# Hash attention with a channel mix: the hash signs of two head pairs made in one PSUM bank

## The chip, the cores and the metric

The kernel runs on one core of a Trainium2 chip. The metric is the device time of one execution in microseconds (us). The engines are named as in the profile: PE is the matrix engine (PEld its weight loads), DVE the vector engine, ACT the scalar engine, POOL the GpSimd engine, SP the engine whose queue issues most transfers; ACTq, POOLq and SPq are the queues of these engines.

## What is computed

The reference has two stages. The first is attention over 4 batches, 8 heads, 768 tokens and 64 values a head, with a hash mask: q and k are projected on 6 directions, the 6 signs make a bucket, and a query sees only keys of its own bucket.

```python
q_bits = (np.einsum('bhsd,dk->bhsk', q, proj) > 0)      # 6 signs
mask = q_bucket[:, :, :, None] == k_bucket[:, :, None, :]
scores = np.where(mask, scale * np.matmul(q, k.transpose(0, 1, 3, 2)), -1000000000.0)
attn = softmax(scores);  out = np.matmul(attn, v)
```

The second is a channel mix over the 512 columns of all heads: each token is mixed with the one before it (`xk`, `xr`), then `k = relu(xk @ w_k)`, `v = (k*k) @ w_v`, `r = sigmoid(xr @ w_r)`, and the output is `r * v`. In what follows "FFN" is this second stage.

## The kernel before

**Pairs, slots, and the order of work.** Two heads of one batch are a pair: 16 pairs, numbered 0 to 15, four to a batch. A pair has 12 slots: for each of its heads j, 6 chunks of 128 keys. The loop over G (line 714) writes the order of all engines out by hand, with n the pair and s its slot: a score of the chunk (`score`, line 421: two matmuls of 384 columns into PSUM, one exp on ACT that writes `pt`), the PV product of the chunk two slots back (`pv`, line 442, six matmuls into `oo`), then half of the slot's FFN work, then what the slot has of side work, then the other half of the FFN work. FFN work is a queue of single matmuls with costs, fed at a fixed rate (`ffn`, line 630); the FFN of a batch begins in slot 5 of the fifth pair (pairs 4, 8, 12) and its outputs leave some three to four pairs later. `later(k, fn)` puts work off to the beginning of the slot k further on. Every engine works off its own instructions in this order, so one that waits holds up all behind it on the same engine, and SP's queue is such a queue too.

**How the mask gets into the scores.** The signs, as +0.5 and -0.5, stand as 6 more rows under the 64 rows of q and k (tiles `aq` and `ak`, called `au` in the code, 70 rows), so that the score matmul adds a term that is greatest for equal buckets. Three sets of these tiles turn round over the pairs (`NSET`, line 199).

**From q and k to signs, for pairs 6 to 15.** Pairs 0 to 5 are loaded and turned in another way (`load_qk`, `turn`, `bits`, with signs at line 388 and their transfers at line 394), which the change leaves as it is. For pairs 6 to 15, four steps count:

- `load_blocks(n + 3)` (line 259) in slot 1 of pair n (slot 3 in pair 4, slot 6 in pair 3): 16 transfers on SP, issued at lines 271, into one of two buffers `blk`; `load_v` (line 278) stands just ahead of it. A `blk` buffer comes free when the squares on ACT (`norm`, line 287, slots 8 and 10 of the pair before) have read it.
- `turn_blocks(n + 2)` (line 326): one transpose for q and one for k on DVE (line 330) into `tq` and `tk`, one buffer each, and four casts on POOL (lines 340 and 342) into the 64 upper rows of `aq` and `ak`. It is done in slots 4 and 5 of pair n, or 6 and 7 where n is a multiple of four.
- `bits_blocks(n + 2, "A")` (line 350) in slot 10 of pair n: four matmuls in 32-bit floats with the projection `projp` as weights, each into 32 rows of a PSUM bank; the rows of head j stand at 6j in a group of 32. `projp` holds the projection twice: for the upper 64 rows in columns 0 to 5, for the lower 64 in columns 6 to 11.
- Its `rest`, at the beginning of slot 11: one comparison on DVE from the bank into `sg` (line 366) and eight transfers on SP (line 371) of six rows each into `aq` and `ak`. The first score that reads them comes 13 slots after the block.

**Banks.** Two PSUM tiles of two banks take scores by turns; four more banks, A to D, take all else. From pair 4 on, C and D belong to the FFN, A and B to the two heads' outputs `oo`: A from slot 2 to 7 of a pair, B from slot 8 to slot 1 of the next. In between, `turn_out` (line 473, slot 3) turns the output of the pair before with six PE transposes into bank B, DVE copies it out into `xt` (line 480), and a shifted column block is copied within `xt` on POOL (line 485; on DVE for the last pair of a batch). The mix of tokens (`mix`, line 490, on DVE) reads `xt` in slots 8 and 9 (slot 4 at a batch's end). Bank A holds the sign block in slots 10 and 11.

Of the kernel before, what the change touches and what calls it, by code (L numbers as in the profile page):

```python
# [9 lines left out]
FP32 = mybir.dt.float32  # L10
BF16 = mybir.dt.bfloat16
# [5 lines left out]
P = 128  # L17
# [12 lines left out]
def kernel(  # L30
# [13 lines left out]
    nc = tc.nc  # L44
    B, H, S, D = q.shape
    NB = proj.shape[1]
# [3 lines left out]
    HALF = S // 2  # L50
    NDC = DM // P
    NFC = DF // P
    NPB = H // 2
    NPAIRS = B * NPB
    AUG = D + NB

    consts = ctx.enter_context(tc.tile_pool(name="consts", bufs=1))
# [5 lines left out]
    nc.vector.memset(epsm, EPS)  # L63
    expb = consts.tile([P, 1], FP32, name="expb")
    nc.vector.memset(expb, EXP_BIAS)
    projp = consts.tile([P, 32], FP32, name="projp")
    nc.vector.memset(projp, 0.0)
    nc.scalar.dma_start(out=projp[0:D, 0:NB], in_=proj)
    nc.vector.tensor_copy(projp[D:P, NB : 2 * NB], projp[0:D, 0:NB])
    make_identity(nc, ident16)  # L70
# [97 lines left out]
    def fast():  # L168
        with ExitStack() as fx:
            pool = lambda nm, bufs, **kw: fx.enter_context(  # L170
                tc.tile_pool(name=nm, bufs=bufs, **kw)
            )

            NKEEP = NPB + 2
            nat = pool("nat", 1)
            blkp = pool("blk", 2)
            turnp = pool("turn", 1)
            vfp = pool("vf", 3)
            sgp = pool("sg", 2)
            sqp = pool("sq", 1)  # L180
            vap = pool("va", 1)
            ptp = pool("pt", 6)
            obp = pool("ob", 2)
            rcp = pool("rc", 4)
            xtp = pool("xt", 1)
# [13 lines left out]
            NSET = 3  # L199
            augs = []  # L200
# [26 lines left out]
            def later(k, fn):  # L227
                due.append((clock[0] + k, len(due), fn))
# [120 lines left out]

            def bits_blocks(n, which):  # L350

                au = augs[n % NSET]
                groups = [(side, e) for e in range(2) for side in "qk"]
                bb = bank(which, [P, HALF], FP32, f"bb{n}")
                for g, (side, e) in enumerate(groups):
                    nc.tensor.matmul(  # L356
                        bb[32 * g : 32 * g + 32, :],
                        projp,
                        turned[n, side][:, e * HALF : (e + 1) * HALF],
                        start=True,  # L360
                        stop=True,
                    )

                def rest():
                    sg = sgp.tile([P, HALF], BF16, name=f"sg{n}", tag="sg")
                    nc.vector.tensor_scalar(
                        out=sg, in0=bb, scalar1=0.0, scalar2=0.5, op0=ALU.is_gt, op1=ALU.subtract
                    )
                    for j in range(2):
                        for g, (side, e) in enumerate(groups):  # L370
                            nc.sync.dma_start(
                                out=au[side, j][D:AUG, e * HALF : (e + 1) * HALF],
                                in_=sg[32 * g + NB * j : 32 * g + NB * j + NB, :],
                            )

                later(1, rest)

            def bits(n, js, which, two_queues=False):
                au = augs[n % NSET]
# [19 lines left out]
            def values(n, j):  # L399
                vf = vfs[n][:, j, :]  # L400
                va, vs = vsets[n % NSET][j]
                if n < NSET:
                    nc.gpsimd.memset(va[:, :, D : D + 1], 1.0)
                    nc.gpsimd.memset(vs[:, D : D + 1], float(NC_))
                if n < NKEEP:
                    nc.gpsimd.tensor_copy(
                        va[:, :, 0:D].rearrange("p (e c) d -> p e c d", e=2),
                        vf.rearrange("p (c e d) -> p e c d", e=2, d=D),
                    )
                else:  # L410
                    nc.gpsimd.tensor_copy(
                        va[:, :, 0:D], vf.rearrange("p (c d) -> p c d", d=D)
                    )
                s3 = sgp.tile([P, 3 * D], FP32, name=f"s3{n}_{j}", tag="s3")
                nc.gpsimd.tensor_add(s3, vf[:, 0 : 3 * D], vf[:, 3 * D : 6 * D])  # L415
                nc.gpsimd.tensor_add(s3[:, 0:D], s3[:, 0:D], s3[:, D : 2 * D])
                nc.gpsimd.tensor_add(vs[:, 0:D], s3[:, 0:D], s3[:, 2 * D : 3 * D])
                vas[n, j], vss[n, j] = va, vs
# [268 lines left out]
                out=mu_rows[NDC : 2 * NDC, :], in_=moe_mu_r.rearrange("(c p) -> c p", p=P)  # L687
            )
            values(0, 0)
            turn(1, 0, 0, "B")  # L690
            turn(1, 1, 0, "D")
            values(0, 1)
# [21 lines left out]
            for G in range(nslots + LAG):  # L714
                clock[0] = G
                n, s = divmod(G, 12)
                live = G < nslots
                run_due()

                if live and s == (5 if n == 0 else 6 if n == NPB - 1 else 3 if n <= NPB else 1):  # L720
                    if NPB <= n < NPAIRS - 2:
                        load_v(n + 2)
                    if n + 3 < NPAIRS:
                        (load_qk if n + 3 < NKEEP else load_blocks)(n + 3)
                    if n < NPB:
                        load_v(n + 2)
                w = weights.get(n, {}).get(s)
                if w:
                    if w[0] == "v":
                        load_wv(w[1])  # L730
                    else:
                        load_w(*w)
                old = chunks[G - LAG] if G >= LAG else None
                first = old is not None and old[2] == 0
                if live:
                    score(*chunks[G])
                if old and not first:
                    pv(*old, oo_bank(*old[:2]))
                rate = 25.9 / (NPB * 12 + (3 if n >= NPAIRS - NPB else 0))
                ffn(rate / 2)  # L740
                mb = misc_bank(n, s)
                if live:
                    if n == 0:
                        if s in (0, 1):
                            turn(1, s, 1, "BD"[s])
                    if n == 1 and s == 0:
                        mups = bank(mb, [P, 2 * NDC], FP32, "mups")
                        nc.tensor.transpose(mups, mu_rows, ident32[0 : 2 * NDC, 0 : 2 * NDC])
                        nc.vector.tensor_copy(mu_sb, mups)
                    if s == (3 if n == 0 else 1) and n + 1 < NKEEP:  # L750
                        bits(n + 1, (0, 1), mb)
                    if s == 10 and NKEEP <= n + 2 < NPAIRS:
                        bits_blocks(n + 2, "A")
                    if s == 3 and n >= 1:
                        turn_out(n - 1, mb)
                    if n >= NPB:
                        if s == 4 and n % NPB == 0:
                            mix((n - 1) // NPB, (n - 1) % NPB, 0)

                        if s in (8, 9) and n % NPB:  # L760
                            mix((n - 1) // NPB, (n - 1) % NPB, 0, [(0,), (1, 2)][s - 8])

                    ms = (5, 7, 9) if n == NPB - 1 else (6, 8, 10)
                    if s in ms and 1 <= n < NPB:
                        mix(0, n - 1, 0, [ms.index(s)])

                    xs = [NPB * 12 + x for x in (5, 10, 11, 12)]
                    if G in xs:
                        mix(0, xs.index(G), 1)
                    if n > NPB and s == (10 if n % NPB else 5):  # L770
                        mix((n - 1) // NPB, (n - 1) % NPB, 1)
                    if s in (5, 7, 9, 11) and n + 2 < NKEEP:
                        x = (s - 5) // 2
                        turn(n + 2, x % 2, x // 2, mb)
                    ts = (6, 7) if n % NPB == 0 else (4, 5)
                    if s in ts and NKEEP <= n + 2 < NPAIRS:
                        turn_blocks(n + 2, ts.index(s))
                    vs_ = (6, 10) if n < NPB else (0, 2)
                    if s in vs_ and n + 1 < NPAIRS:
                        values(n + 1, vs_.index(s))  # L780
                    if s in (8, 10) and NKEEP <= n + 2 < NPAIRS:
                        norm(n + 2, (s - 8) // 2)
                ffn(rate / 2)
                if old and first:
                    pv(*old, oo_bank(*old[:2]))
                if live and n >= NPB and n % NPB == 0 and s == MIXSLOT - 1:
                    queue.extend(ffn_items(n // NPB - 1))
# [178 lines left out]
    with tc.manual_schedule():  # L966
        fast()
# [33 lines left out]
```

## Time and profile before

| What | Value |
|---|---|
| median of 3 runs | 267.44 us (266.5 to 267.85) |
| the profiled execution | 267.24 us |
| its span, first to last instruction | 265.4 us |
| mean granted PE clock | 0.996 of full speed |
| first score of pair 0 / 5 / 6 / 7 / 8 | 12.3 / 68.7 / 84.4 / 98.6 / 113.3 us |
| first score of pair 9 / 11 / 13 / 15 | 127.9 / 157.1 / 186.2 / 213.2 us |
| moved over the span | 36.50 MB, 138 GB/s |

Times within an execution count from the span's start. The span falls into a start-up of 12.3 us, four pairs without FFN work (some 11 us each), pairs 4 to 15 with it, and an end of some 40 us after pair 15 in which the last batch's FFN runs alone. In the profile, each instruction is named by its engine, line and operation, with the tiles that it writes and reads, as in `bb<-tq,projp`; a busy matrix engine is not one at its peak, as its instructions overlap. A "wait" names the instruction whose end let a waiting engine go on.

### The profile page before, as it was taken

Reading aid. Unit: us, or ns where it says so; the run is one execution under the profiler, and the core shown is the slowest. Engines: PE = TensorE matmul, PEld = TensorE weight load, DVE = VectorE, ACT = ScalarE, POOL = GpSimd, SP = SyncE. Lnnn points to the kernel's source line nnn. Section 1 sums busy time; section 2 is a strip of 40 time slices with the busy share of each in tenths; the row PEclk is TensorE's granted clock in tenths of the full one; section 3 lists DMA queues with packets and bytes.
Section 4 is the critical chain, followed back from the end, with each engine's and each line's share of the span. In section 5 each row is a group of like instructions: output and inputs, shape, how many; then the busy total and the mean of one; then the engine's idle time right before and its main releaser. Section 6 shows DMA issues by size and latency. Waiting matters only on the chain.

```text
span 265.4 us, 6612 instructions
## 1 busy us (share of the span) xinstructions
PE 248.4 (94%) x2411; PEld 150.1 (57%) x2441; DVE 186.0 (70%) x378; ACT 213.8 (81%) x318; POOL 124.5 (47%) x248
## 2 busy tenths in 40 slices
PE   7799999999989999999999999998999999989990
PEld 5366657566555655565565656564656666545450
DVE  3667689889898775759588776778596645776440
ACT  2099979799989998979999997988999988179700
POOL 5787597770999471913665484706392000000000
PEclk9999999999999999999999999999999999999998
DMA  6548685857759292959665391959510002220042
GB/s 218 201 85 165 246 311 124 252 120 168 188 113 240 37 236 50 245 151 235 169 168 115 86 199 51 220 183 227 133 59 8 2 2 82 79 79 0 19 148 86
DMA packets 25976, 36.50 MB, mean 138 GB/s; under 512 B 3144, under 2 KB 21136, under 8 KB 25936
## 3 DMA queue, kind: packets, MB, share of 16 engines
q1 hardware_dynamic: 24008, 32.45, 47.2%
q0 software_dynamic: 1536, 3.15, 5.3%
q8 instruction: 21, 0.34, 0.6%
q10 hardware_dynamic: 392, 0.40, 0.5%
q14 instruction: 19, 0.16, 0.2%
HBM read 30.68 MB, written 6.29 MB: 139 GB/s over the span
## 4 chain that ended last, share of the span: by engine, by line
PE 56%; DVE 14%; DMA 11%; ACT 7%; SPq 5%; issue 4%; ACTq 0%; DVEq 0%
PE vp L529 14%; PE sc L427 13%; PE kp L529 10%; PE oo L454 7%; PE rp L529 5%; ACT pt L434 5%; DMA blk<-in_k_dram 4%; SPq L394 3%; DMA qk<-in_k_dram 3%; DMA qk<-in_q_dram 2%; PE bb L356 2%; PE ot L479 2%; SPq L271 2%; DVE xk L511 2%; DMA blk<-in_q_dram 2%
## 5 line engine op out<-in xcount | busy, mean ns | idle before, releaser
L434 ACT ACTIVATE pt<-sc,expb 128x768 bf16<-128x768 f32 x192 | 166.2, 909 | 26.3 <-PE sc L427 15.8
L427 PE MATMUL sc<-aq,ak 70*128 70x384 bf16 x384 | 93.9, 325 | 2.4 <-DMA aq<-sg 0.3
L454 PEld LDWEIGHTS <-pt 128*128 128x128 bf16 x1152 | 60.5, 97 | 26.7
L454 PE MATMUL oo<-va,pt 128*128 128x65 bf16 x1152 | 66.3, 193 | 0.0
L529 PE MATMUL kp<-xk,wk_sb 128*128 128x384 bf16 x256 | 55.6, 325 | 2.2 <-DVE kr L554 1.1
L427 PEld LDWEIGHTS <-ak 70*128 70x128 bf16 x384 | 34.9, 98 | 28.7 <-issue 7.4
L529 PE MATMUL vp<-wv_sb,k 128*128 128x512 bf16 (+1 forms) x187 | 48.9, 370 | 0.4
L561 DVE TENSOR_TENSOR k<-kr 128x384 bf16<-128x384 bf16 x64 | 28.5, 460 | 6.6 <-ACT kr L552 6.1
L529 PEld LDWEIGHTS <-wk_sb 128*128 128x128 bf16 x256 | 21.7, 97 | 14.3 <-issue 4.0
L340 POOL CAST aq<-tq 64x768 bf16<-64x768 f32 x20 | 16.6, 832 | 23.4 <-PE sc L427 11.7
L529 PE MATMUL rp<-wr_sb,xr 128*128 128x512 bf16 x79 | 24.5, 379 | 0.7 <-issue 0.2
L552 ACT ACTIVATE kr<-kp 128x384 bf16<-128x384 f32 x36 | 18.1, 503 | 7.4 <-PE kp L529 7.4
L529 PEld LDWEIGHTS <-k 128*128 128x128 bf16 x200 | 16.8, 97 | 12.8 <-issue 2.7
L485 POOL COPY xt<-xt 128x127 bf16<-128x127 bf16 x12 | 3.5, 294 | 41.8 <-DVE xt L480 41.8
L415 POOL TENSOR_TENSOR s<-vf 128x192 f32<-128x192 f32 x32 | 22.0, 688 | 0.0
L593 DVE SCALAR_TENSOR_TENSOR os<-th,vp 128x512 f32<-128x512 bf16 (+1 forms) x25 | 16.5, 662 | 6.9 <-PE vp L529 5.8
L465 DVE RECIPROCAL rc<-oo 128x6 f32<-128x6 f32 x32 | 6.1, 190 | 20.5 <-PE oo L454 20.5
L480 DVE COPY xt<-ot 128x768 bf16<-128x768 bf16 x16 | 8.9, 557 | 16.0 <-PE ot L479 16.0
L554 DVE TENSOR_SCALAR kr<-kp 128x384 bf16<-128x384 f32 x28 | 15.4, 550 | 6.3 <-PE kp L529 6.1
L466 DVE TENSOR_TENSOR ob<-oo,rc 128x384 bf16<-128x384 f32 x32 | 17.8, 557 | 1.1
L342 POOL TENSOR_SCALAR ak<-tk 64x768 bf16<-64x768 f32 x20 | 17.1, 854 | 2.8 <-DVE tk L330 1.3
L298 ACT ACTIVATE sq<-blk 128x768 bf16<-128x768 f32 x20 | 17.0, 852 | 0.0
(72 smaller groups left out, 308.2 us busy)
## 6 DMA issues: line engine op xcount, KB each, us to landing
blk<-in_q_dram SPq DMA_DIRECT2D x40, 176.0 KB
blk<-in_k_dram SPq DMA_DIRECT2D x40, 176.0 KB
vf<-in_v_dram SPq DMA_DIRECT2D x16, 384.0 KB
out_dram<-os SPq DMA_DIRECT2D x23, 256.0 KB
wvs<-in_moe_w_v_dram SPq DMA_DIRECT2D x4, 512.0 KB
qk<-in_q_dram SPq DMA_DIRECT2D x3, 384.0 KB
qk<-in_k_dram SPq DMA_DIRECT2D x3, 384.0 KB
aq<-sg SPq DMA_DIRECT2D x64, 4.5 KB
```

The source lines that it names most:

```text
L298: nc.scalar.activation(junk.rearrange("p (u d) -> p u d", u=NTOK), blks[n][:, i, :, 0:32], AF.Square, scale=1.5, accum_out=nrm[:, i, n : n ...
L340: eng.tensor_copy(dst, src)
L342: eng.tensor_scalar(out=dst, in0=src, scalar1=ALPHA, scalar2=1.0, op0=ALU.mult, op1=ALU.mult,)
L415: nc.gpsimd.tensor_add(s3, vf[:, 0 : 3 * D], vf[:, 3 * D : 6 * D])
L427: nc.tensor.matmul(sc[:, sp, 0:HALF], au["k", j][:, jc * P : (jc + 1) * P], au["q", j][:, sp * HALF : (sp + 1) * HALF], start=True, stop=True,
L434: nc.scalar.activation(pt.rearrange("p (s q) -> p s q", s=2), sc[:, :, 0:HALF], AF.Exp, bias=expb, scale=SCALE,)
L454: nc.tensor.matmul(oo[:, ic, :], pts[n, j, jc][:, ic * P : (ic + 1) * P], vas[n, j][:, jc, :], start=False, stop=(jc == NC_ - 1 and ic == ...
L466: nc.vector.tensor_tensor(out=obs[n][:, :, j * D : (j + 1) * D], in0=oo[:, :, 0:D], in1=rc.to_broadcast([P, NC_, D]), op=ALU.mult,)
L529: nc.tensor.matmul(box["t"], lhs(), rhs(), start=(i == 0), stop=(i == len(mms) - 1))
L552: nc.scalar.activation(kr, kp, AF.Relu)
L561: lambda: nc.vector.tensor_tensor(out=k2, in0=kr, in1=kr, op=ALU.mult),
L593: nc.vector.scalar_tensor_tensor(out=os_, in0=mx["th", b, c][:, ms], scalar=1.0, in1=vp, op0=ALU.add, op1=ALU.mult,)
```

## The change

There is a second weight tile `projq`, zero but for columns 16 to 27, which hold what `projp` has in columns 0 to 11. In slot 5 of an odd pair n, `bits_blocks(n + 1)` makes the signs of pairs n+1 and n+2 in bank B: four matmuls with `projp` for pair n+1, then four with `projq` for pair n+2 that add to the same bank, so that the second pair's rows stand 16 further down in each group of 32. There is one comparison for both, at the beginning of slot 6, followed by the eight transfers of pair n+1; those of pair n+2 follow in two lots of four, 5 and 9 slots after the block. For that, `turn_blocks(n + 2)` moves to slots 1 and 2 where n is odd; where n is even it stays. The buffers of `tq` and `tk` are doubled, those of `vf` go from three to two and those of `pt` from six to five.

```diff
     projp = consts.tile([P, 32], FP32, name="projp")
+    projq = consts.tile([P, 32], FP32, name="projq")
     nc.vector.memset(projp, 0.0)
+    nc.vector.memset(projq, 0.0)
...
-            turnp = pool("turn", 1)
-            vfp = pool("vf", 3)
+            turnp = pool("turn", 2)
+            vfp = pool("vf", 2)
...
-            ptp = pool("pt", 6)
+            ptp = pool("pt", 5)
...
             def bits_blocks(n, which):
 
-                au = augs[n % NSET]
+
                 groups = [(side, e) for e in range(2) for side in "qk"]
                 bb = bank(which, [P, HALF], FP32, f"bb{n}")
-                for g, (side, e) in enumerate(groups):
-                    nc.tensor.matmul(
-                        bb[32 * g : 32 * g + 32, :],
-                        projp,
-                        turned[n, side][:, e * HALF : (e + 1) * HALF],
-                        start=True,
-                        stop=True,
-                    )
+                for m in range(2):
+                    for g, (side, e) in enumerate(groups):
+                        nc.tensor.matmul(
+                            bb[32 * g : 32 * g + 32, :],
+                            (projp, projq)[m],
+                            turned[n + m, side][:, e * HALF : (e + 1) * HALF],
+                            start=(m == 0),
+                            stop=(m == 1),
+                        )
+                sg = sgp.tile([P, HALF], BF16, name=f"sg{n}", tag="sg")
 
                 def rest():
-                    sg = sgp.tile([P, HALF], BF16, name=f"sg{n}", tag="sg")
                     nc.vector.tensor_scalar(
                         out=sg, in0=bb, scalar1=0.0, scalar2=0.5, op0=ALU.is_gt, op1=ALU.subtract
                     )
-                    for j in range(2):
-                        for g, (side, e) in enumerate(groups):
-                            nc.sync.dma_start(
-                                out=au[side, j][D:AUG, e * HALF : (e + 1) * HALF],
-                                in_=sg[32 * g + NB * j : 32 * g + NB * j + NB, :],
-                            )
+                    send(0, 0)
+                    send(0, 1)
+
+                def send(m, j):
+                    au = augs[(n + m) % NSET]
+                    for g, (side, e) in enumerate(groups):
+                        r0 = 32 * g + 16 * m + NB * j
+                        nc.sync.dma_start(
+                            out=au[side, j][D:AUG, e * HALF : (e + 1) * HALF],
+                            in_=sg[r0 : r0 + NB, :],
+                        )
 
                 later(1, rest)
+                later(5, lambda: send(1, 0))
+
+                later(9, lambda: send(1, 1))
...
             values(0, 0)
+            nc.gpsimd.tensor_copy(projq[:, 16:28], projp[:, 0:12])
...
-                    if s == 10 and NKEEP <= n + 2 < NPAIRS:
-                        bits_blocks(n + 2, "A")
...
-                    ts = (6, 7) if n % NPB == 0 else (4, 5)
+                    ts = (1, 2) if n % 2 else (6, 7) if n % NPB == 0 else (4, 5)
                     if s in ts and NKEEP <= n + 2 < NPAIRS:
                         turn_blocks(n + 2, ts.index(s))
+                    if s == 5 and n % 2 and NKEEP <= n + 1 < NPAIRS:
+                        bits_blocks(n + 1, mb)
```

## The prediction

> **What bounds the kernel now.** I read the page first, then busy time by stage, then the timelines of TensorE, VectorE and SyncE around the sign blocks, and last the waits.
>
> ```profile
> PE 248.4 (94%) x2411; PEld 150.1 (57%) x2441; DVE 186.0 (70%) x378; ACT 213.8 (81%) x318; POOL 124.5 (47%) x248
> ```
>
> TensorE fills 94% of the span and ScalarE 81%, but those are averages. By pair (columns: stretch, length, then busy us of PE, PEld, DVE, ACT, POOL, the clock, DMA) it looks so for pairs 5, 6 and 7:
>
> ```profile
> 68.70:84.40 15.70, 14.55 (x147) 8.60 (x148) 15.40 (x27) 14.91 (x27) 14.50 (x25) 1.00 0.87 196
> 84.40:98.60 14.20, 14.04 (x145) 8.53 (x147) 10.98 (x23) 14.00 (x23) 8.77 (x17) 1.00 0.65 142
> 98.60:113.30 14.70, 14.42 (x142) 8.20 (x143) 9.43 (x17) 13.20 (x19) 8.42 (x16) 1.00 0.71 154
> ```
>
> From pair 6 on PE is busy for 96 to 99% of a pair (92% in pair 12) and decides its length, with ACT close behind where FFN phases give it relus and tanhs. VectorE has some 3 to 5 us to spare per pair. Pair 5 is the exception: DVE 15.40 and POOL 14.50 of 15.70 us, and here PE waits for DVE (0.9 us at the transposes of the output, 1.3 us counted by their weight loads). So what the change takes from DVE is worth something only in pair 5, and what it adds ahead of a PE wait costs most there.
>
> **The merged block on PE.** One old sign block, in the PE timeline (start, us, engine, line, operation):
>
> ```profile
> 110.85 0.38 PE L529 MATMUL vp<-wv_sb,k 128*128 128x512 bf16 x1
> 111.16 0.51 PE L356 MATMUL bb<-tq,projp 128*32 128x384 f32 x1
> ...
> 111.51 0.49 PE L356 MATMUL bb<-tk,projp 128*32 128x384 f32 x1
> ...
> 111.94 0.39 PE L529 MATMUL vp<-wv_sb,k 128*128 128x512 bf16 x1
> ```
>
> Four matmuls leave eight records in two passes, at 111.16 and 111.51: the four 32-row groups run side by side. A vp matmul holds PE for about 0.215 us (two from 109.91 to the score at 110.34), so entry costs 111.16 - 110.85 - 0.215 = 0.095 us, a pass 0.35, the last pass with the exit 0.43: 0.87 us a block. Two blocks are 1.75 us; one merged block of four passes is 0.095 + 3 x 0.35 + 0.43 = 1.58. The number of matmuls is the same (40), so the merger saves only one entry and one exit, **0.17 us for two pairs**; accumulating the second group on the first is not in the trace: between nothing and one more pass gap of 0.1 us, and I take nothing.
>
> **VectorE, small things.** Five sign comparisons of 546 ns go (L366, mean), 2.7 us of DVE work, hidden beside PE in all pairs but 5. The second projection's memset (0.085 us, as L67) and its POOL copy (0.1 to 0.3 us, by the 0.10 of a memset and the 0.29 of L485) lie in the start-up, under loads that DVE waits 3.6 us for: nothing. Five pt buffers for six: exp G writes the buffer of chunk G-5, whose PV stands on PE before the score of G, which exp G waits for anyway: nothing. Two vf buffers for three: load_v(n+2) now waits for values(n), not values(n-1). Closest is vf7, wanted by SP at about 71.2 us; values(5,1) ends on POOL at 70.5. Nothing.
>
> **Transfers on SP.** The 80 sign transfers stay 80. Eight of them hold SP's queue for about 6 us, and in before they stand ahead of the next loads:
>
> ```profile
> 71.18 0.70 SPq L371 DMA_DIRECT2D aq<-sg  x1
> ...
> 77.04 0.67 SPq L371 DMA_DIRECT2D ak<-sg  x1
> 77.81 0.39 SPq L281 DMA_DIRECT2D vf<-in_v_dram  x1
> 78.31 1.82 SPq L271 DMA_DIRECT2D blk<-in_q_dram  x4
> ```
>
> In the new order, loads of odd pairs have no signs ahead and move up by about 6 us; even pairs have twelve ahead (slots 6 to 14 of the odd pair) and keep about their place. A block load takes 9 to 10 us from issue to landing (issued from 105.04; the next pairs likewise), so turning at slots 1 and 2 finds its data landed, with one exception below. What becomes tight is the first lot: the even pair's signs are now made six slots before use, not thirteen. From the block's end: 0.4 us to the comparison and 0.57 for it (112.34 to 112.91), three more issues at 0.75, and 2.0 us to land (the chain of waits has 2.02 for ak<-sg): 5.2 us, against 6.9 us to the next pair's first score (105.76, slot 6 of pair 7, to 113.33 less the old block's 0.87, plus 0.2 for the rest of slot 5). The reserve of 1.7 us holds unless DVE is late; the second lot has 6 slots more, the third nearly 12.
>
> **Turning at slots 1 and 2.** Two transposes (0.97 us each) now stand on DVE ahead of the xt copy of slot 3, which frees bank B for the new block at slot 5. DVE idles before that copy for 1.44 us in pair 7, 1.35 in 9, 1.44 in 11 and 0.90 in 13, and transposes hold it about 1.8 us together, so xt ends 0.4 to 0.9 us later, still 0.4 to 0.9 us before PE asks for the bank (in pair 7: xt ends at 104.2, slot 5 starts at 104.81 and its block stands half a slot later). On POOL, the four casts (0.83 and 0.85 us) move ahead of values(n+1,1) and of the xt column copy, where POOL now idles (4.6 us in pair 7); the copy then ends about 4 us later, near 108.4, as the mix of slot 8 (107.9 plus the 0.7 us that the merged block has added) asks for it. Nothing, with up to 0.5 us a pair kept for the range.
>
> The trace has DVE squares (L561, two SBUF inputs) from 316 to 982 ns, the long ones where POOL works without a break. The Trainium skill (SBUF — State Buffer, Who interferes with whom) speaks against the move: an instruction with two SBUF inputs and a GpSimd instruction that reads SBUF exclude each other, and the loser waits out the other. By that rule up to three squares a pair would wait 0.8 us each, behind casts that now run in slots 2 to 5; they leave slots 5 to 8, so the sum by it is again about zero.
>
> **Pair 5 is where it costs.** Its block load for pair 7 is held up by unchanged work (eight signs of pair 5 on SP until 66.7 us). It is issued from 67.35 and landed at 76 us, which busy time of the DMA engines shows (next to last column: DMA share):
>
> ```profile
> 74.00:76.00 2.00, 1.54 (x17) 1.11 (x19) 2.00 (x5) 1.31 (x3) 1.86 (x4) 1.00 1.06 204
> 76.00:78.00 2.00, 2.00 (x24) 1.29 (x23) 1.94 (x3) 2.00 (x4) 1.77 (x5) 1.00 0.04 7
> ```
>
> And DVE's order there now is:
>
> ```profile
> 73.79 0.56 DVE L466 TENSOR_TENSOR ob<-oo,rc 128x384 bf16<-128x384 f32 x1
> 74.26 0.92 DVE L561 TENSOR_TENSOR k<-kr 128x384 bf16<-128x384 bf16 x2
> 75.11 0.55 DVE L480 COPY xt<-ot 128x768 bf16<-128x768 bf16 x1
> 75.57 0.96 DVE L330 STREAM_TRANSPOSE tq<-blk 128x768 f32<-128x768 f32 x1
> 76.47 0.62 DVE L561 TENSOR_TENSOR k<-kr 128x384 bf16<-128x384 bf16 x1
> 77.14 0.98 DVE L330 STREAM_TRANSPOSE tk<-blk 128x768 f32<-128x768 f32 x1
> ```
>
> In the new order: ob ends 0.47 earlier (no comparison at 68.97), at 73.9; tq to 74.85; a square to 75.3; then tk waits for the k half until 76.0, ends at 77.0; a square; xt ends at 78.0. PE, which is at slot 5's block at 76.45 (76.9 less 0.47), waits 1.6 us for bank B, and the next slot starts at 78.05 + 3 x 0.35 + 0.43 + 0.2 = 79.7, against 77.12: +2.6. The block of slot 10 is gone, -0.87, which leaves +1.7 if PE sets the rest of the pair. But ACT is busy from 76.8 to 84.4 almost without a gap (4.10 of 4.20 us, then 2.00 of 2.00 twice), and its exp of slot 6 moves by 2.4: by ACT it is +2.4. I take **+2.2**, nearer to ACT, as its rows are full.
>
> **Sum.** Pair 5 +2.2 (its own merger is in it); four mergers -0.7; in pairs 6 and 10 ACT (14.00 of 14.20, 13.90 of 14.50) can't follow all of the 0.87 us that leaves PE; exps in a row take 0.82 and not 0.91, so ACT's floor is up to 1.1 us below its busy time and the loss between 0 and 0.7 each; I take 0.25, +0.5. Together +2.0. The profiled execution took 267.24 us (span 265.4 and 1.84 around it): 269.2; the median of the three runs is 0.2 above that execution, so I say 269.3.
>
> **Rivals.** *Pair 5's wait is hidden* (0.27): the forecast turns on tk ahead of xt; if the k half is there before DVE, or the bank comes free by 76.45, the 1.6 us vanish. Then -0.9 (five mergers) to +0.8: 266.3 to 268.0, not slower. For it: DVE may be earlier than 73.9. Against: the DMA share stays above 1 until 76. *VectorE's relief counts* (0.13): place: PE's waits that DVE ends in pairs 5, 8 and 12 (0.9 to 1.3 at ot, 0.9 at kp in 12, 0.7 at old blocks); price: half of some 3 us and the mergers, -2.4, about 265. It decides once DVE is a comparison earlier (0.5 us) where PE waits; against: in pair 12 mixing, not signs, delays kr. *Every odd pair stalls* (0.15): bank B, the mix waiting for POOL, or the first lot of signs, each short by 0.5 to 1 us, four times on top of the forecast: 271 to 273. *The forecast* has 0.45, 268.2 to 270.3.
>
> The change does what it says, by the code: the same signs, fewer comparisons.
>
> **Chances.** 0.5% (1.34 us), about what a measurement can tell, puts the bounds at 266.1 and 268.8. The forecast is slower for 0.36 of its 0.45, the stalls all 0.15: 0.51. Faster: 0.11 of the relief and 0.02 of the hidden case, 0.13. The rest, 0.36. Range 266.0 to 272.0.
>
> **What would show it.** Right: a DVE wait for blk ahead of tk near 75 us, a PE wait of 1 to 2 us before the first sign block, pair 6's first score near 86.6 instead of 84.4, later odd pairs longer by about 0.7 us and even ones shorter by as much; blk issued right after the norms in even pairs. Wrong: sign blocks of 16 records that take over 1.7 us, scores that wait for aq<-sg at the start of pairs 6, 8, 10, 12 or 14, mixes that wait for POOL.

## The result

The changed kernel took 274.56 us (median of 6 runs, 273.66 to 276.31) against 267.40 us for the kernel before (6 runs, 266.50 to 269.67): a ratio of 1.026 (95% interval 1.021 to 1.031). It is slower by 2.6%. The forecast was 269.3 us, slower by 0.7%, with a range of 266.0 to 272.0: the direction was right, the size was not. The profiled execution took 274.54 us (span 272.6, mean granted clock 0.993), 7.3 us more than that of before.

The first score of pair 6 comes at 86.85 us (84.43 before), that of pair 15 at 220.19 (213.16 before). So pair 5 accounts for 2.4 us, pairs 6 to 14 for 4.6 us (133.34 against 128.73), and everything after pair 15's start for 0.2 us. The forecast had +2.2 for pair 5 and -0.2 for pairs 6 to 14: **the second is what was missed**.

### The profile after

The engines' line and the two groups that changed, from the page (columns of a group: busy us, mean ns of one, idle us of the engine ahead of them and what ended it):

```profile
PE 249.3 (91%) x2411; PEld 150.8 (55%) x2441; DVE 182.9 (67%) x374; ACT 213.4 (78%) x318; POOL 121.9 (45%) x249
...
L446 ACT ACTIVATE pt<-sc,expb 128x768 bf16<-128x768 f32 x192 | 165.9, 909 | 33.7 <-PE sc L439 32.2
L439 PE MATMUL sc<-aq,ak 70*128 70x384 bf16 x384 | 93.9, 325 | 5.1 <-ACT pt L446 2.4
```

PE and ACT have the work that they had (249.3 us against 248.4, 213.4 against 213.8), in a longer span. The waits of the two for each other have grown: ACT waits 32.2 us for scores, 8.7 of them once, before the first score (15.8 before, where the first wait, 8.9 us, is put down to another engine), and PE waits 2.4 us for exps at the scores (0.2 before).

Busy time of pairs 5, 6 and 7, as it was shown for before:

```profile
68.77:86.85 18.08, 15.58 (x156) 8.94 (x156) 15.71 (x28) 14.51 (x25) 15.49 (x29) 1.00 0.87 183
86.85:101.16 14.31, 13.61 (x138) 8.45 (x139) 10.00 (x20) 14.12 (x23) 6.08 (x9) 1.00 0.67 160
101.16:116.97 15.81, 15.07 (x150) 8.47 (x151) 9.01 (x17) 12.88 (x18) 8.81 (x18) 1.00 0.51 129
```

Pair 6 has lost its sign block and PE is 0.43 us less busy than before, yet it is 0.12 us longer. Pair 7 is 1.1 us longer, for a block that is only some 0.6 us longer than the old one.

**Pair 5 went by the chain that the forecast had, with other sizes in it.** VectorE's order in it (start, us, line, operation, then the idle time before and its releaser):

```profile
74.34 0.56 DVE L478 TENSOR_TENSOR ob<-oo,rc 128x384 bf16<-128x384 f32 x1
74.81 0.97 DVE L333 STREAM_TRANSPOSE tq<-blk 128x768 f32<-128x768 f32 x1
75.70 0.32 DVE L573 TENSOR_TENSOR k<-kr 128x384 bf16<-128x384 bf16 x1
76.44 0.98 DVE L333 STREAM_TRANSPOSE tk<-blk 128x768 f32<-128x768 f32 x1 [0.42 <-DMA blk<-in_k_dram]
77.34 0.47 DVE L573 TENSOR_TENSOR k<-kr 128x384 bf16<-128x384 bf16 x1
77.74 0.54 DVE L492 COPY xt<-ot 128x768 bf16<-128x768 bf16 x1
```

The second transpose waits for the k half of the load, and the copy that frees bank B ends at 78.28 (78.0 in the forecast). PE then goes on:

```profile
78.33 0.51 PE L360 MATMUL bb<-tq,projp 128*32 128x384 f32 x1 [0.83 <-DVE xt L492]
...
79.77 0.50 PE L541 MATMUL kp<-xk,wk_sb 128*128 128x384 bf16 x2
80.10 0.49 PE L439 MATMUL sc<-aq,ak 70*128 70x384 bf16 x2
```

PE stood from 77.5 to 78.33, and slot 6 begins at 80.10 (79.7 in the forecast). That wait of 0.83 us is half of the 1.6 in the forecast; but PE reached the block at 77.50 and not at 76.45, as the division of the output (the first line above) ended at 74.90, 0.55 us later than in the kernel before (74.35) and not 0.47 earlier.

**The block of 16 records**, in pair 9 on PE, one line of each pass:

```profile
138.45 0.51 PE L360 MATMUL bb<-tq,projp 128*32 128x384 f32 x1
...
138.80 0.49 PE L360 MATMUL bb<-tq,projp 128*32 128x384 f32 x1
...
139.12 0.49 PE L360 MATMUL bb<-tq,projq 128*32 128x384 f32 x1
...
139.45 0.49 PE L360 MATMUL bb<-tq,projq 128*32 128x384 f32 x1
...
139.88 0.50 PE L541 MATMUL kp<-xk,wk_sb 128*128 128x384 bf16 x2
```

From 138.45 to 139.88 are 1.43 us, with the entry about 1.5 (1.58 in the forecast). Adding the second group on the first costs nothing that can be seen: the passes are 0.32 to 0.35 us apart, against 0.35 in an old block.

### Where pairs 6 to 14 lost 4.6 us

Pairs are the wrong stretch to look at. The old block stood in slot 10, the new one stands in slot 5, so the busy time is taken from the score of slot 8 to that of slot 2 of the next pair, for pairs 6 to 13. In the kernel before (columns as above: stretch, length, busy us of PE, PEld, DVE, ACT, POOL, clock, DMA):

```profile
93.36:101.05 7.69, 7.46 (x73) 3.98 (x73) 4.40 (x11) 7.69 (x14) 4.61 (x10) 1.00 1.03 223
107.86:115.43 7.57, 7.47 (x72) 4.05 (x73) 5.84 (x11) 7.18 (x11) 5.10 (x9) 1.00 1.08 248
122.30:130.22 7.92, 7.58 (x77) 4.34 (x76) 5.92 (x12) 7.60 (x14) 6.01 (x11) 1.00 1.06 234
137.35:144.61 7.26, 7.21 (x75) 4.19 (x75) 7.02 (x15) 7.26 (x13) 5.20 (x11) 1.00 0.81 163
151.65:159.22 7.57, 7.52 (x74) 4.08 (x74) 6.20 (x12) 7.57 (x13) 6.19 (x12) 1.00 0.90 197
166.03:173.17 7.14, 7.09 (x70) 3.87 (x71) 5.22 (x11) 6.58 (x11) 4.52 (x9) 1.00 1.10 216
180.09:188.24 8.15, 7.10 (x75) 4.16 (x75) 5.20 (x12) 7.36 (x13) 6.71 (x13) 1.00 1.08 247
195.00:202.33 7.33, 7.15 (x74) 4.15 (x74) 6.22 (x15) 7.33 (x14) 5.34 (x10) 1.00 0.01 3
```

In the changed kernel:

```profile
96.35:104.05 7.70, 6.73 (x65) 3.91 (x65) 4.21 (x10) 7.70 (x14) 3.31 (x5) 1.00 0.60 141
112.39:119.18 6.79, 6.74 (x65) 3.91 (x65) 4.90 (x10) 6.75 (x11) 2.52 (x6) 1.00 0.13 46
126.05:133.97 7.92, 7.11 (x69) 4.19 (x68) 5.81 (x12) 7.61 (x14) 5.02 (x8) 1.00 0.88 221
142.43:149.66 7.23, 6.79 (x68) 4.10 (x67) 5.19 (x14) 7.23 (x13) 2.83 (x8) 1.00 0.03 6
156.73:164.31 7.58, 6.89 (x66) 4.00 (x66) 5.56 (x11) 7.58 (x13) 4.09 (x7) 1.00 0.53 137
172.65:179.15 6.50, 6.36 (x64) 3.72 (x63) 4.44 (x10) 6.24 (x11) 2.61 (x6) 1.00 0.13 46
186.07:193.72 7.65, 6.59 (x67) 4.01 (x67) 5.02 (x11) 7.13 (x13) 5.12 (x8) 1.00 0.88 220
202.01:209.35 7.34, 6.48 (x65) 4.00 (x66) 5.39 (x12) 7.34 (x14) 2.33 (x7) 1.00 0.04 9
```

Look at the ACT column. In pairs 6, 9, 10 and 13 ACT is busy for the whole stretch before and after (7.69 of 7.69 and 7.70 of 7.70, and so on), and in pair 8 for all but the same 0.3 us. These five stretches are as long as they were (within 0.03 us), although 0.87 us of PE work has left each: six exps, the FFN's relus and tanhs and the two squares of slots 8 and 10 fill ACT, and the old sign block lay on PE beside the squares at no cost. Only where ACT had room did the stretch get shorter: by 0.78 us in pair 7, 0.64 in pair 11, 0.50 in pair 12. In all, eight blocks left and 1.93 us came back (60.65 to 58.72).

From slot 2 to slot 8 of an odd pair it is the other way round. Pair 7 before and after:

```profile
101.05:107.86 6.81, 6.76 (x71) 4.15 (x71) 4.30 (x8) 5.39 (x7) 2.76 (x4) 1.00 0.33 95
```

```profile
104.05:112.39 8.34, 8.23 (x86) 4.55 (x86) 4.79 (x9) 5.45 (x7) 6.29 (x13) 1.00 0.85 213
```

PE is full (6.76 of 6.81) and ACT has over 1.3 us to spare, so the new block costs all of its time: +1.53 us here, +5.92 in the four odd pairs, 1.48 a block. ACT stands idle there. Its row beside the block in pair 9:

```profile
137.38 1.79 ACT L446 ACTIVATE pt<-sc,expb 128x768 bf16<-128x768 f32 x2
140.81 0.90 ACT L446 ACTIVATE pt<-sc,expb 128x768 bf16<-128x768 f32 x1 [1.63 <-PE sc L439]
```

5.92 paid, 1.93 returned: +3.99. With slots 0 to 8 of pair 6 (+0.57, PE waiting for ACT after pair 5's late squares) and 0.05 elsewhere, this is the 4.61 us.

### The profile page after: what moved, and what is told of

Its sections match the earlier page's. It is cut to its first block, busy times and chain, and to the rows that moved or that the text cites. A ratio compares the mean times of both kernels' runs of the same rounds, so it can differ in the third digit from the quotient of the medians.

```text
span 272.6 us, 6615 instructions
## 1 busy us (share of the span) xinstructions
PE 249.3 (91%) x2411; PEld 150.8 (55%) x2441; DVE 182.9 (67%) x374; ACT 213.4 (78%) x318; POOL 121.9 (45%) x249
## 4 chain that ended last, share of the span: by engine, by line
PE 46%; DMA 19%; ACT 13%; SPq 8%; DVE 6%; issue 5%; ACTq 0%; POOL 0%; DVEq 0%
PE vp L541 11%; PE sc L439 10%; ACT pt L446 9%; PE kp L541 9%; PE oo L466 5%; DMA blk<-in_k_dram 5%; PE rp L541 4%; SPq L274 4%; DMA blk<-in_q_dram 3%; SPq L406 3%; DMA qk<-in_k_dram 3%; PE bb L360 3%; DMA ak<-sg 3%; ACT sq L301 2%; DMA aq<-sg 2%
## 5 line engine op out<-in xcount | busy, mean ns | idle before, releaser
L446 ACT ACTIVATE pt<-sc,expb 128x768 bf16<-128x768 f32 x192 | 165.9, 909 | 33.7 <-PE sc L439 32.2
L427 POOL TENSOR_TENSOR s<-vf 128x192 f32<-128x192 f32 x32 | 20.9, 652 | 0.0
```

What stands on the lines that cost most here:

```text
L446: nc.scalar.activation(pt.rearrange("p (s q) -> p s q", s=2), sc[:, :, 0:HALF], AF.Exp, bias=expb, scale=SCALE,)
```

## Experiments

**Theory A**: the time is lost between PE and ACT, by the place of the block relative to the squares: a PE block beside ACT's squares is free, and one where ACT has nothing of its own is paid in full. **Theory B**, the rival: the transposes in slots 1 and 2, with VectorE and GpSimd behind them, delay the odd pairs. Beside the ratio, each run is read by four numbers of its profiled execution (us): the first score of pair 6, which tells pair 5's cost, roughly; the eight stretches from slot 8 to slot 2 added up ("ends"); the four from slot 2 to 8 of pairs 7, 9, 11, 13 ("odd middles"); and the span.

| Kernel | ratio to before (95%) | pair 6 begins | ends | odd middles | span |
|---|---|---|---|---|---|
| before | 1 | 84.43 | 60.65 | 27.50 | 265.4 |
| changed | 1.026 (1.021-1.031) | 86.85 | 58.72 | 33.42 | 272.6 |
| 1 odd squares in the block | 1.011 (1.006-1.015) | 86.44 | 56.75 | 33.42 | 269.5 |
| 2 turning alone | 1.000 (0.997-1.003) | 85.78 | 60.65 | 27.49 | 267.4 |
| 3 pair 5 as before | 1.017 (1.013-1.022) | 84.75 | 58.72 | 33.42 | 269.6 |
| 4 before, squares early | 1.009 (1.006-1.013) | 85.94 | 60.49 | 28.86 | 269.8 |
| 5 before, no squares | 0.991 (0.987-0.994) | 83.96 | 60.07 | 27.56 | 264.4 |
| 6 changed, no squares | 1.000 (0.997-1.003) | 88.21 | 53.22 | 33.57 | 268.0 |
| 7 all squares in the block | 1.013 (1.008-1.018) | 87.85 | 56.03 | 34.14 | 271.0 |
| 8 as 7, pair 5 as before | 1.002 (0.999-1.005) | 85.31 | 56.03 | 34.14 | 268.3 |
| 9 two single blocks | 1.021 (1.015-1.026) | 86.67 | 60.14 | 30.84 | 270.3 |
| 10 place alone | 1.008 (1.005-1.012) | 87.29 | 59.19 | 31.06 | 270.3 |
| 11 squares where ACT has room | 0.998 (0.994-1.001) | 84.69 | 53.91 | 33.56 | 265.2 |

The ratios are to the kernel before, run again beside each experiment: its median was 268.96 us beside 1 to 4, 268.22 beside 5 to 8 and 267.84 beside 9 to 11. The expectations were made from 267.4 us, so each is held against the ratio times 267.4. The beginning of pair 6 is that of a single execution and varies: in experiment 4, which differs from the kernel before only after it, it comes 1.5 us later. In the profiled executions of 6, 7 and 10 the clock fell in pair 5 (last section), which lengthens that column and the span, but not ends and odd middles.

### 1. The odd pairs' squares moved to the block

The changed kernel, with both squares of an odd pair in slot 5.

```diff
-                    if s in (8, 10) and NKEEP <= n + 2 < NPAIRS:
+                    if s in (8, 10) and n % 2 == 0 and NKEEP <= n + 2 < NPAIRS:
                         norm(n + 2, (s - 8) // 2)
+                    if s == 5 and n % 2 and NKEEP <= n + 2 < NPAIRS:
+                        norm(n + 2, 0)
+                        norm(n + 2, 1)
```

> The changed kernel, with both squares of an odd pair moved from slots 8 and 10 to slot 5, beside the merged sign block. Theory A (ACT starves during the merged block, 1.6 to 2.4 us a time, and falls behind where its two squares stand without a block on PE beside them): the squares fill ACT's hole, the waits of PE at the start of pairs 6, 10, 12 and 14 (0.3 to 0.6 us each in the changed kernel) go, 274.5 falls by 1.0 to 2.5 us, to 272.0 to 273.5; the waits at the start of pairs 7, 9, 11 and 13 stay, as the even pairs' squares stay where they are. Theory B (the transposes in slots 1 and 2 hold up VectorE's copies and evictions): no change, 274.0 to 275.0.

271.44 us: more came back than the 1.0 to 2.5 us expected, 1.5% or 4.1 us by the ratios, 3.1 between the profiled spans. The sum of the odd middles didn't change: the squares are free there. The ends of the even pairs stay as in the changed kernel (but for 0.26 us more in pair 10), those of the odd ones fall. The ends of pairs 6 to 9:

```profile
95.36:103.05 7.69, 6.73 (x65) 3.90 (x65) 4.20 (x10) 7.69 (x14) 3.31 (x5) 1.00 0.66 157
111.39:118.08 6.69, 6.64 (x66) 3.91 (x66) 4.88 (x10) 5.56 (x7) 2.49 (x6) 1.00 0.14 47
124.94:132.86 7.92, 7.12 (x69) 4.19 (x68) 5.82 (x12) 7.61 (x14) 5.00 (x8) 1.00 0.82 204
141.31:147.68 6.37, 6.32 (x67) 4.11 (x67) 5.19 (x14) 6.03 (x9) 2.83 (x8) 1.00 0.03 7
```

Pair 9's end, the fourth line, is 6.37 us instead of 7.23, with PE busy for 6.32 of it. The 0.86 us that the block's departure had left unused is there at once.

### 2. Turning at slots 1 and 2 alone

The kernel before, with the changed buffers and only this:

```diff
-                    ts = (6, 7) if n % NPB == 0 else (4, 5)
+                    ts = (1, 2) if n % 2 else (6, 7) if n % NPB == 0 else (4, 5)
```

> The kernel before with the odd pairs turned in slots 1 and 2 and with the changed numbers of buffers (tq and tk two, vf two, pt five); the sign blocks stay single, in slot 10, in bank A. Theory A: PE waits for nothing new but in pair 5, where the k half of the load is late, and there the delayed xt copy holds no block: 267.0 to 268.5. Theory B: the larger part of the loss, 270 to 273.

268.4 us, no difference, as theory A expected. Ends and odd middles are those of before, to a hundredth; of the even middles, pair 8's is 0.49 us longer. **Theory B falls.** In the profiled execution pair 5 is 1.2 us longer (PE waits 2.1 us for the output's division on VectorE there); the interval, which ends at +0.3%, says that on average less is lost.

### 3. Pair 5 as before

The changed kernel, but pairs 6 and 7 get single blocks in slot 10 of pairs 4 and 5, and pair 7 is turned in slots 4 and 5. (Here and in experiments 8, 9 and 11 `bits_blocks` has a third argument, the number of pairs in a block.)

```diff
-                    ts = (1, 2) if n % 2 else ...
+                    ts = (1, 2) if n % 2 and n > 5 else ...
...
+                    if s == 10 and n in (4, 5):
+                        bits_blocks(n + 2, "A", 1)
-                    if s == 5 and n % 2 and NKEEP <= n + 1 < NPAIRS:
+                    if s == 5 and n % 2 and NKEEP < n + 1 < NPAIRS:
```

> The changed kernel, but pair 7 is turned in slots 4 and 5 of pair 5 and the signs of pairs 6 and 7 are made in single blocks in slot 10 of pairs 4 and 5, in bank A, as before; the merged blocks begin in pair 7. If the late load in pair 5 costs 2.4 us, as the start of pair 6 (86.85 against 84.43) says: 272.1, between 271.6 and 272.6. Rival: most of that delay would have come anyway, as ACT is full in pair 5: above 273.3.

273.0 us, 272.0 by the ratio, as expected. The ratio falls by 0.9%, 2.3 us; pair 6 begins 2.1 us earlier; ends and middles are unchanged. Pair 5's cost is about what the forecast said (the two intervals leave some 1.8 us either way), and it is separate from the rest.

### 4. The old kernel with its squares taken from beside the block

The kernel before, with the squares of pairs 8 to 15 in slots 3 and 5:

```diff
-                    if s in (8, 10) and NKEEP <= n + 2 < NPAIRS:
-                        norm(n + 2, (s - 8) // 2)
+                    ns = (3, 5) if n > 5 else (8, 10)
+                    if s in ns and NKEEP <= n + 2 < NPAIRS:
+                        norm(n + 2, ns.index(s))
```

> The kernel before with the squares of pairs 8 to 15 moved from slots 8 and 10 to slots 3 and 5, away from the sign block of slot 10. Theory A: PE's block no longer gives ACT the time for its squares: ACT waits at slot 10 and PE at slots 4 to 7, slower by 1.0 to 3.5 us, 268.4 to 271. Theory B, in which only VectorE counts: no change, 267.0 to 268.0.

271.52 us, slower by 0.9%, within theory A's range. Sign blocks, turning and transfers are those of before; moving ACT's squares away from the block suffices to lose 2.5 us. The ends gain nothing by it (60.49, as good as without squares in experiment 5: PE with its block bounds them), while the odd middles lose 1.36 us, the even ones (slots 2 to 8 of pairs 8, 10, 12 and 14) 0.85 and slots 0 to 8 of pair 6 0.95. This turns the case round. The loss lies where ACT has no room for the squares: pair 13's middle, here and (second line) in the kernel before:

```profile
191.81:199.40 7.59, 7.13 (x74) 4.44 (x73) 5.97 (x13) 7.59 (x14) 3.63 (x7) 1.00 0.19 58
188.24:195.00 6.76, 6.71 (x74) 4.45 (x74) 5.32 (x10) 6.47 (x10) 2.83 (x6) 1.00 0.28 91
```

In pair 11, where ACT had 1.36 us free, the same move cost nothing. So neither the block nor the squares are dear as such; a stretch is as long as its fuller engine needs.

### 5 and 6. Both kernels without squares

Both leave out the squares of pairs 6 to 15 (line 287 on); the check value that is formed from them then covers pairs 0 to 5 alone. The edit is the same in both:

```diff
+    nc.vector.memset(nrm, 0.0)
...
-                    if s in (8, 10) and NKEEP <= n + 2 < NPAIRS:
-                        norm(n + 2, (s - 8) // 2)
```

> The kernel before without the squares of pairs 6 to 15 (20 of ACT's instructions with their accumulator reads; the bound that the flag stands for is then taken over pairs 0 to 5 alone). The base for the next run. PE sets the pairs from 6 on, so theory A expects little: pair 5, where ACT is full, shorter by up to 1 us, in all 266.0 to 267.4 where before has 267.4.

> The changed kernel without the squares of pairs 6 to 15. Theory A: without squares ACT has time in every pair, so only pair 5's wait (+2.4) and the mergers (-0.7) are left: 1.0 to 2.5 us over the kernel before without squares, 267.5 to 269.5 where before has 267.4. Rival: something other than ACT's share (bank B, the transposes, the sign transfers, a longer block) costs the 4.6 us after pair 5: still 5 us or more over it, 271 or more.

The kernel before without squares took 266.35 us: 0.9% less (0.6 to 1.3), 2.5 us, and so more than the up to 1.4 us expected. Its profiled span is only 1.0 us shorter; where the rest lies isn't shown. The changed kernel without squares took 268.95 us, 2.5 us over the other by the ratios: the upper end of theory A's range, half of the rival's 5. The end of pair 9, old kernel and changed:

```profile
136.53:143.79 7.26, 7.21 (x75) 4.18 (x75) 7.01 (x15) 6.18 (x9) 5.18 (x11) 1.00 0.84 169
141.18:147.55 6.37, 6.32 (x67) 4.11 (x67) 5.21 (x14) 6.08 (x9) 2.83 (x8) 1.00 0.03 7
```

With squares the two were 7.26 and 7.23 us. In the old kernel the squares cost 0.58 us of the ends, beside blocks that PE pays for anyway. In the changed one they cost 5.50 (58.72 to 53.22). Without squares in either, the ends fall by 60.07 - 53.22 = 6.85 us, 0.86 for each of the eight blocks: that is the full return, of which the changed kernel saw 1.93. And over pairs 6 to 14 the changed kernel without squares is 0.84 us *shorter* than the old one without (127.35 against 128.19): the mergers do bring what the forecast gave them (0.7). The run as a whole shows less of it, because pair 5 got longer still (20.4 us in the profiled execution; see the last section).

### 7 and 8. All four squares at the block

Squares of the even pair moved to the odd one too, into slots 4, 5, 5 and 6; there they are taken from the turned tiles, so that each row of the check value adds up other rows. Run 8 has pair 5 as in experiment 3.

```diff
-                        junk.rearrange("p (u d) -> p u d", u=NTOK),
-                        blks[n][:, i, :, 0:32],
+                        junk,
+                        turned[n, "qk"[i]],
...
-                    if s in (8, 10) and NKEEP <= n + 2 < NPAIRS:
-                        norm(n + 2, (s - 8) // 2)
+                    if n % 2 and n > NPB:
+                        for s4, m4, i4 in ((4, 1, 0), (5, 1, 1), (5, 2, 0), (6, 2, 1)):
+                            if s == s4 and NKEEP <= n + m4 < NPAIRS:
+                                norm(n + m4, i4)
```

> The changed kernel with the four squares of both pairs of a block beside that block (slots 4, 5, 5 and 6 of the odd pair), taken from tq and tk and not from blk, which holds the next load's buffer no longer (the same values, summed over other rows for the bound). Theory A: the waits of PE at the start of pairs 7, 9, 11 and 13 (0.80, 1.05, 0.80 and 0.29 us) go as well, PE gets back 0.87 us in each even pair: 1.5 us over before (pair 5 +2.2, mergers -0.7), between +0.7 and +2.5. Rival: it stays where the odd pairs' squares alone brought it, +2.8.

> The same, with pair 5 as before (signs of pairs 6 and 7 in single blocks in slot 10 of pairs 4 and 5, their squares in slots 8 and 10). Theory A: the wait in pair 5 goes, four mergers stay: 0 to 1.5 us under before, the likeliest -0.7. Rival: the merged block costs by itself, +1 or more.

272.82 and 269.23 us, by the ratios 3.6 and 0.6 us over before. Both missed, on the slow side: the first lies nearer to its rival (+2.8), the second between theory A and its rival (+1). Even ends are now free of squares and short (27.51 us for four, as without squares), but odd ends are 28.51, longer than in the changed kernel. Four squares are 3.7 us of ACT; an odd middle has 8.34 - 5.45 = 2.9 us free in pair 7 and 8.46 - 6.45 = 2.0 in pair 9. What does not fit runs on into the end that follows. So the theory holds only as far as ACT has room beside the block, counted in microseconds.

### 9. The changed places without the merger

One single block in slot 5 (bank B) and one in slot 10 (bank A) of each odd pair.

```diff
...
-                        bits_blocks(n + 1, mb)
+                        bits_blocks(n + 1, mb, 1)
+                    if s == 10 and n % 2 and NKEEP <= n + 2 < NPAIRS:
+                        bits_blocks(n + 2, "A", 1)
```

> The changed kernel without the merger: in an odd pair n the signs of pair n+1 in a single block in slot 5 (bank B), those of pair n+2 in a single block in slot 10 (bank A), each with its own comparison and eight transfers. Theory A has two parts: ACT's hole in slot 5 (halved here) and the lost cover of the even pairs' squares (as in the changed kernel). So about half of the 4.6 us after pair 5 comes back: 1.0 to 3.0 us under the changed kernel, 4 to 6 over before. Rival: the length of the merged block alone is to blame: even with the kernel before but for pair 5, +2 to +3.

272.54 us, by the ratios 5.5 us over before and 1.4 under the changed kernel, as theory A expected (the two intervals overlap). Odd middles fall by 2.58 us against the changed kernel, while the odd ends, where the block now stands beside the squares again, grow by 1.44 (27.87 to 29.31). Splitting the merged block and putting one half back beside the squares *saves* about 1.1 us there, though it adds an entry and an exit.

### 10. The place alone

The kernel before, with only the odd pairs' own single block moved from slot 10 to slot 5 (from pair 7 on, turned in slots 1 and 2); the even pairs keep theirs in slot 10, and the buffers are as changed.

```diff
-                    if s == 10 and NKEEP <= n + 2 < NPAIRS:
+                    early = n % 2 and n > 5
+                    if s == 10 and not early and NKEEP <= n + 2 < NPAIRS:
                         bits_blocks(n + 2, "A")
...
+                    if s == 5 and early and NKEEP <= n + 2 < NPAIRS:
+                        bits_blocks(n + 2, mb)
```

> The kernel before with the odd pairs 9, 11, 13 and 15 turned in slots 1 and 2 and their single sign block moved from slot 10 (bank A) to slot 5 (bank B); the even pairs, and pair 5's part, as before; buffers as changed. The place alone, without a merger. Theory A: pairs 7, 9, 11 and 13 lose the cover of their squares, as in the run with early squares (there +0.63 in pair 9 and +0.83 in pair 13, nothing in 7 and 11): +1.0 to +2.5 us over before. Rival: a single block costs the same in any slot: within 0.5 us of before.

270.19 us, slower by 0.8%, 2.2 us, within theory A's range, with no merger and the same work. Odd middles +3.56 us (four blocks of 0.89), ends -1.46: pairs 7 and 11 give back 0.78 and 0.64, pairs 9 and 13 0.04 and nothing. Its profiled execution had a slower clock in pair 5, so its span says less than its ratio.

### 11. Squares moved to where ACT has room

Experiment 3 (pair 5 as before), with the squares of odd pairs in slot 5, beside the block, and those of even pairs in slots 2 and 6. All of the computation is there.

```diff
-                    if s in (8, 10) and NKEEP <= n + 2 < NPAIRS:
-                        norm(n + 2, (s - 8) // 2)
+                    ns = (8, 10) if n < 6 else (5, 5) if n % 2 else (2, 6)
+                    for i4 in range(2):
+                        if s == ns[i4] and NKEEP <= n + 2 < NPAIRS:
+                            norm(n + 2, i4)
```

> The merged block with pair 5 as before and squares placed for it: both squares of an odd pair in slot 5, beside the block, those of an even pair in slots 2 and 6 in place of 8 and 10 (from pair 6 on). All is computed. Theory A: no hole and no backlog at the end of even pairs, so the mergers' -0.7 comes through, less what ACT lacks in pairs 6 and 10: between -1.0 and +0.8 us against before. Rival: the mergers cost, +2 or more.

267.31 us against 267.84, a ratio of 0.998 (0.994 to 1.001): within theory A's range. The loss is gone, and against the kernel before nothing is measurable. The ends of pairs 6 to 9:

```profile
93.85:100.81 6.96, 6.73 (x66) 3.97 (x65) 3.76 (x10) 6.96 (x12) 2.94 (x5) 1.00 1.07 228
109.14:115.83 6.69, 6.58 (x65) 3.91 (x65) 4.94 (x10) 5.57 (x7) 2.52 (x6) 1.00 0.17 62
122.69:129.80 7.11, 6.81 (x70) 4.20 (x69) 5.54 (x11) 6.54 (x10) 5.01 (x8) 1.00 1.01 255
138.39:144.76 6.37, 6.32 (x67) 4.11 (x67) 5.26 (x14) 6.03 (x9) 2.83 (x8) 1.00 0.03 7
```

All eight are within 0.7 us, in all, of those without squares (53.91 against 53.22). The even pairs' squares stand beside no block here, yet the even middles are as long as before (27.49 us): ACT has room there for squares set apart. From slot 8 of pair 6 to slot 8 of pair 14 this kernel needs 114.96 us, the kernel before 115.64: 0.68 us less, what four mergers were worth in the forecast. That is about all that the change had to give, a quarter of a percent.

## Why the prediction was wrong, step by step

- **The step that failed** is the third term of the sum: "in pairs 6 and 10 ACT (14.00 of 14.20, 13.90 of 14.50) can't follow all of the 0.87 us that leaves PE; ... the loss between 0 and 0.7 each; I take 0.25, +0.5". The loss was 6.85 - 1.93 = 4.9 us over eight stretches, up to all of the 0.86 in each, and it lay in the odd pairs 9 and 13 as much as in even ones. Behind it stands the reading of the first view: "From pair 6 on PE is busy for 96 to 99% of a pair ... and decides its length". That is an average. Pair 10 is 13.90 of 14.50 for ACT, but from its slot 8 to slot 2 of pair 11 ACT is busy 7.57 of 7.57 us. The floor estimate from "exps in a row" (up to 1.1 us below the busy time) does not hold there: those five shrank by 0.03 us at most.
- **Moving and merging were priced as one.** "Four mergers -0.7" is right (0.84 without squares, 0.68 in experiment 11). But a move is two prices: 1.48 a block where it goes, and what ACT lets back where it leaves. "Later odd pairs longer by about 0.7 us and even ones shorter by as much" came out as +1.11, +1.73, +1.44, +1.81 (pairs 7, 9, 11, 13) and +0.12, -0.78, -0.29, -0.64, +0.14 (pairs 6, 8, 10, 12, 14).
- **Pair 5 was right in size, in part by luck**: +2.2 said, +2.3 measured (18.08 against 15.75 us), by the chain named (transpose waits for k, copy late, PE waits for bank B); experiment 3 returned 2.3 us. But two terms were off and cancel: the wait was 0.83 us and not 1.6, and VectorE, and PE with it, came some half a microsecond later than in the kernel before, where the forecast had it 0.47 earlier. Why VectorE was late wasn't tried. The k half was there 0.4 us later than read (76.4, not 76.0), and slot 6 began 0.4 us later than said.
- **The merged block** was right (1.58 said, about 1.5). **Transfers** were right: no score from pair 6 on waits for signs by more than 0.4 us, and in odd pairs the loads move up (issued 1.1 us into pair 7, at 102.30, against 6.4 us into it before); in even pair 8 they stand 4.2 us into the pair, not right behind the squares as the signs to watch had it.
- **Turning at slots 1 and 2** was right at nothing (experiment 2), outside pair 5. Neither bank B after pair 5 nor the mixes stalled anyone: the one wait of a mix for POOL is 0.4 us, as before. The Trainium skill (SBUF — State Buffer, Who interferes with whom) would have made the FFN's squares on VectorE (`k<-kr`) wait for the casts; no run here shows a price for it in the later pairs (over the whole run one took 457 ns on average, 460 before).
- **The rivals.** "Every odd pair stalls" was nearest in size (271 to 273) and wrong in each of its three mechanisms. The rival that was missing is "the block is free where it stands", with ACT's full rows in slots 8 to 1 as its place and 0.86 a block as its price; it could have been read from the trace of before, since the first fence of ends above is from there.

## What to carry to other kernels

Before moving work between places of a pipeline, take busy time over the stretch that it leaves and over the one that it enters, not over a whole period: two engines that are 94% and 81% busy on average can each be the bound, in turns. Work on one engine is free while the other is full, and leaving such a place returns nothing; it is paid in full where its own engine is full. If work must move, place its partner anew too: with pair 5 as before, squares beside the block or where ACT has room turned +1.7% (experiment 3) into no difference (experiment 11).

## What the runs showed of the hardware

In some executions PE's granted clock fell to half in pair 5, after short idle times. In experiment 6, PE stood idle from 76.0 to 78.4 us, waiting for the copy; 0.7 us after it went on, a pass of the block took 0.64 us instead of 0.33, and busy time by two microseconds (the clock is the third column from the end) shows:

```profile
76.00:78.00 2.00, 0.00 (x0) 0.00 (x0) 1.34 (x3) 0.77 (x1) 1.15 (x3) 1.00 1.08 289
78.00:80.00 2.00, 1.60 (x16) 0.50 (x16) 0.77 (x2) 0.00 (x0) 1.87 (x4) 0.76 1.09 215
80.00:82.00 2.00, 2.00 (x12) 0.77 (x9) 0.56 (x1) 0.00 (x0) 1.84 (x7) 0.50 1.09 215
82.00:84.00 2.00, 2.00 (x22) 1.26 (x20) 1.27 (x4) 1.53 (x2) 1.84 (x6) 0.89 0.68 141
```

In experiment 10 a PE busy for 0.39 of the two microseconds from 74 was followed by a clock of 0.60 and 0.55 in the next four; its longest wait there was 1.74 us. In experiment 2 the same stretch, with 0.25 busy and a wait of 2.07 us, was followed by none:

```profile
74.00:76.00 2.00, 0.25 (x5) 0.26 (x6) 1.93 (x5) 0.97 (x2) 1.41 (x3) 1.00 0.77 149
76.00:78.00 2.00, 1.95 (x25) 1.26 (x24) 2.00 (x4) 1.10 (x2) 1.25 (x2) 1.00 0.03 7
```

From the block's start to the first score of pair 6 experiment 6 took 9.8 us (78.40 to 88.21), the changed kernel at full clock 8.5 (78.33 to 86.85): by an estimate from these two the fall cost some 1.3 us on top of the wait, or more, since ACT has no squares to do in experiment 6. In experiments 6 and 10 the rows add up to 1.70 us of clock lost, which is half speed for 3.4 us. Such a fall does not follow every wait. The Trainium skill (TensorE: Matmul & The Clock Gate, Part 1: The HAM clock gate) says that the clock goes to half after an idle window of about 3.4 us, and that the window runs freely. That it depends on the moment agrees with these runs; that 3.4 us of idleness are needed does not, as 2.4 us and 1.74 us did it here. The profiled execution of the changed kernel had no such fall (clock 1.00 throughout pair 5). What decides when it comes was not tried.
